# One written list of steps for the first batch of an attention and MLP kernel, and fewer transfers for v and the keys

## The chip, the cores and the metric

The kernel runs on one core of a Trainium2 chip. The metric is device microseconds of one execution, the median over runs. Lower is better. A profiled execution gives, besides its own time, a trace of every instruction of every engine: TensorE (PE; PEld is its weight load), VectorE (DVE), ScalarE (ACT), GpSimd (POOL), and SyncE (SP), which here only issues DMAs. A letter q behind an engine's name (SPq, POOLq) means the engine's own instruction queue issuing a DMA.

## The reference

Attention over q, k, v of shape (8 batches, 12 heads, 448 positions, 64), with each query and key row divided by its root mean square and multiplied by a gain, then a two-layer network with a tanh gelu over the 3584 x 768 result:

```python
def rmsnorm(x, g):
    rms = np.sqrt(np.mean(x * x, axis=-1, keepdims=True) + 1e-06)
    return x / rms * g
q_n, k_n = (rmsnorm(q, g_q), rmsnorm(k, g_k))
scores = (1.0 / np.sqrt(64)) * np.matmul(q_n, k_n.transpose(0, 1, 3, 2))
scores = scores - np.max(scores, axis=-1, keepdims=True)
attn = np.exp(scores)
attn = attn / (np.sum(attn, axis=-1, keepdims=True) + 1e-09)
attn_out = np.matmul(attn, v)
x = attn_out.transpose(0, 2, 1, 3).reshape(3584, 768)
h = x @ w_in                                    # w_in 768 x 2048
g = 0.5 * h * (1.0 + np.tanh(c * (h + 0.044715 * h * h * h)))
out = g @ w_out                                 # w_out 2048 x 768
```

Inputs and output are float32; the kernel multiplies in bfloat16. Instead of each row's maximum it subtracts a constant (`shift`) that it computes from the gains.

## The kernel before, in words

The order of the instructions of every engine is the order in which the code emits them (`manual_schedule`, L69); each engine takes its own in that order, and waits for others come from the tiles that instructions share. A tile that is taken from a pool waits until everything that uses the pool's same buffer before it is over.

**Units.** A batch's 12 heads form six pairs, two heads to a pair (`head`, L103), and two pairs form one of three chunks. A chunk's queries and keys come in one raw tile each (`load_q`, `load_k`, L106 and L122, SP issues, six DMAs in all). 448 keys make three full tiles of 128 keys for each pair and a rest of 64 keys; the rests of the two pairs of a chunk share one tile ("r"). So a batch has 21 score tiles. Before, each pair's heads have 256 keys (four to a partition) on their own 64 partitions and 192 keys (three to a partition) on the other 64 (`halves`, L117). v goes the same way through POOL with a cast to bfloat16 (`load_v`, L139): three DMAs for each half of the heads, where the third (`vr`) writes the rest rows once more into a tile of their own.

**A pair's way.** Squares (L164, on ACT or POOL), totals along the 64 columns (DVE, L192), reciprocal root on ACT (`rsqrt`, L195, a logarithm and an exponential), normalization (L209, on DVE or POOL), transposition on PE into a PSUM tile (`trans`, L221), copies to `qT` and `kT` (DVE); or, for later batches, transposition by DMA (L248) and a gain on DVE (L260). Then `scores` (L265): two matmuls and one exponential of ACT for each tile. `pair_products` (L306) with what=0 gives the sums of exponentials (by a weight of ones), with what=1 the product with v. `pair_recips` (L326) transposes the sums on DVE, takes the reciprocal and transposes back; `pair_x` (L335) multiplies into `xT`.

**PSUM.** Three tiles of two banks (`ps_s`, for scores and pairs of first-layer blocks), one bank `ps_o` (`bank`, for sums and products), one bank `ps_m` (for transpositions, single first-layer blocks, and the second layer).

**First batch.** Loads, memsets and 16 idle matmuls on zeros (L620), the first pair's steps written out (L621 to L650), then `first_attention` (L514): a loop over the 21 tiles, with steps hung on tile numbers in four plans (`side`, `mid`, `early`, `late`, L661 to L680). Sums and products of a pair take turns in the one bank of `ps_o`. At its end `first_blocks` (L496) mixes the last pair's sums with the first first-layer blocks, calls `between0` (L701: the rest of batch 1's totals, its reciprocal roots in one go, and the load of the gelu table), and the remaining blocks of the first layer (`mm1`, L349) follow; between them batch 1 is normalized on DVE, pairs 0, 1, 4 and 5 are transposed on PE and chunk 1 by DMA (plan `m1`, L713).

**Later batches.** `attention` (L451) runs batch b + 1 in seven groups of three tiles, each filled up with steps of the second layer of batch b (`FILLS`, 96 steps after the first batch, the first 48 of which need the first half of `wout` alone); then `first_blocks` and the first layer of batch b + 1, while batch b + 2 is loaded, squared, normalized on POOL and transposed by DMA. POOL issues the weights' loads (`w_in_part`, two halves; `w_out_part`, two halves). Raw tiles have four buffers for each kind; a placeholder tile is taken once (L565).

## Time and profile before

| what | us |
|---|---|
| median of 3 runs (range) | 434.73 (434.52 to 435.49) |
| profiled execution, its own time | 437.02 |
| its span, first to last instruction | 434.9 |
| PE / ACT / DVE / POOL busy in the span | 414.1 / 286.1 / 265.4 / 160.6 |
| 0 to 100 us: PE busy, mean of ten stages | 83.8 of 100 |
| 100 to 435 us: PE busy | 330.3 of 335 |

The span is what the trace covers; sums over the trace are made against it. The share of busy time is a mean over stages with different limits: the first 100 us and the rest have to be read apart. A line of the timeline gives start, duration, engine, source line, operation, output and inputs with shapes, how many are merged, and in brackets the idle time before and what ended it. DMA moved at 178 to 242 GB/s in each of the first eight stages of 10 us and at 124 to 131 between 150 and 250 us. Loads issued at 25 to 31 us took 16.4 to 16.8 us to land, those of the first 4 us between 2.4 and 4.0.

### The profile page before, as it was taken

What the parts mean: (1) busy time and instruction counts of PE and PEld (TensorE: products, weight loads), DVE (VectorE), ACT (ScalarE), POOL (GpSimd) and SP (SyncE); (2) the same over time, 40 slices, a digit from 0 to 9 for tenths busy, and PEclk for the clock granted to TensorE, in tenths of its full rate; (3) what the DMA queues carried; (4) which work ended last, traced back from release to release, by engine and by line L of the source; (5) the groups of instructions that cost most, each with busy time, mean ns of one, the idle gap of its engine ahead of it and who ended that gap; (6) DMA issues with size and microseconds to landing.
All of it is one profiled execution on the core that took longest, in us unless ns stands there. A gap on an engine that the chain in (4) does not pass through costs nothing.

```text
span 434.9 us, 9265 instructions
## 1 busy us (share of the span) xinstructions
PE 414.1 (95%) x3776; PEld 236.4 (54%) x3776; DVE 265.4 (61%) x441; ACT 286.1 (66%) x382; POOL 160.6 (37%) x181
## 2 busy tenths in 40 slices
PE   8778798899999999999999999999999999999996
PEld 3234454456555565556465655556565655556563
DVE  5577846798667844787267845877377821784010
ACT  5676538366787758767786859777786648674400
POOL 4979223254660094205560194206560280000000
PEclk9899999699999999999999999999999999999999
DMA  7999999665895158913994168914991162120022
GB/s 177 217 228 233 231 179 230 124 110 95 206 194 107 38 128 170 217 51 73 208 186 102 38 150 160 217 43 78 220 142 39 38 110 56 36 69 7 2 72 72
DMA packets 90505, 54.92 MB, mean 126 GB/s; under 512 B 51808, under 2 KB 85472, under 8 KB 90464
## 3 DMA queue, kind: packets, MB, share of 16 engines
q1 hardware_dynamic: 65248, 41.67, 42.9%
q0 software_dynamic: 24896, 12.59, 21.9%
q8 instruction: 29, 0.48, 0.4%
q10 hardware_dynamic: 320, 0.10, 0.1%
q14 instruction: 12, 0.10, 0.1%
HBM read 47.19 MB, written 11.01 MB: 134 GB/s over the span
## 4 chain that ended last, share of the span: by engine, by line
PE 79%; DMA 13%; DVE 5%; SPq 2%; issue 1%; ACT 0%; DVEq 0%
PE o L386 32%; PE hh L362 26%; PE o L321 10%; PE sc L285 6%; DMA rawk<-in_k_dram 6%; DMA rawq<-in_q_dram 4%; PE h L362 3%; DMA kT<-nrmk 3%; PE sc L275 1%; SPq L129 1%; DVE ss L193 1%; DVE es L301 1%; DVE es L299 1%; SPq L110 1%; DVE nrmq L216 0%
## 5 line engine op out<-in xcount | busy, mean ns | idle before, releaser
L386 PE MATMUL o<-wout,g 128*64 128x384 bf16 (+1 forms) x1664 | 159.7, 329 | 0.0
L289 ACT ACTIVATE ex<-sc,shift 128x896 bf16<-128x896 f32 x144 | 136.6, 1013 | 8.5 <-PE sc L285 8.4
L362 PE MATMUL hh<-xT,win 128*64 128x448 bf16 (+1 forms) x960 | 135.3, 355 | 2.7 <-ACT g L368 2.6
L386 PEld LDWEIGHTS <-g 128*64 128x64 bf16 (+1 forms) x1664 | 99.4, 110 | 50.6 <-issue 4.6
L362 PEld LDWEIGHTS <-win 128*64 128x64 bf16 (+1 forms) x1098 | 88.1, 106 | 61.5 <-issue 8.2
L368 ACT ACTIVATE g<-hh 128x896 bf16<-128x896 f32 x56 | 49.6, 917 | 55.0 <-PE hh L362 55.0
L193 DVE TENSOR_REDUCE ss<-sq 112x16 f32<-112x1024 f32 (+4 forms) x44 | 46.8, 1077 | 39.9 <-ACT sq L176 32.7
L408 ACT COPY osb<-o 128x384 f32<-128x384 f32 x51 | 24.7, 485 | 59.5 <-PE o L386 59.5
L331 DVE STREAM_TRANSPOSE st<-o 128x448 f32<-128x448 f32 x48 | 31.2, 649 | 29.4 <-PE o L321 29.3
L654 POOL COPY mark<-es 1x1 bf16<-1x1 bf16 x6 | 1.1, 178 | 127.0 <-DVE es L301 127.0
L216 POOL TENSOR_TENSOR nrmq<-rawq,rinv 112x512 bf16<-112x512 f32 x40 | 41.7, 1060 | 3.1 <-ACT rinv L202 3.1
L285 PE MATMUL sc<-qT,kT 64*128 64x448 bf16 x288 | 38.6, 355 | 1.4 <-DVE kT L243 0.9
L321 PE MATMUL o<-ex,vb 128*64 128x448 bf16 x288 | 36.9, 363 | 1.0 <-DVE st L331 0.8
L301 DVE TENSOR_TENSOR es<-ex 128x896 bf16<-128x896 bf16 x42 | 27.7, 659 | 15.4 <-ACT ex L289 15.2
L216 POOL TENSOR_TENSOR nrmk<-rawk,rinv 128x384 bf16<-128x384 f32 (+1 forms) x40 | 36.8, 936 | 0.0
L338 DVE TENSOR_TENSOR xT<-o,rb 128x448 bf16<-128x448 f32 x48 | 29.6, 617 | 4.4 <-PE o L321 3.5
L178 POOL TENSOR_TENSOR sq<-rawq 112x1024 f32<-112x1024 f32 x9 | 17.4, 1929 | 39.9 <-DMA rawq<-in_q_dram 25.8
L333 DVE STREAM_TRANSPOSE rb<-rc 128x448 f32<-128x448 f32 x48 | 31.0, 645 | 1.6
L299 DVE TENSOR_TENSOR es<-es,exr 64x896 bf16<-64x896 bf16 x42 | 27.4, 653 | 3.0 <-ACT exr L289 1.6
L301 DVE TENSOR_TENSOR es<-es,ex 128x896 bf16<-128x896 bf16 x42 | 27.1, 645 | 2.4 <-ACT ex L289 0.3
L261 DVE TENSOR_SCALAR kT<-kT,gcol 128x896 bf16<-128x896 bf16 x19 | 15.4, 813 | 21.4 <-DMA kT<-nrmk 21.4
L289 ACT ACTIVATE exr<-sc,shift 128x896 bf16<-128x896 f32 x24 | 24.5, 1021 | 0.2 <-PE sc L275 0.2
(71 smaller groups left out, 318.4 us busy)
## 6 DMA issues: line engine op xcount, KB each, us to landing
rawq<-in_q_dram SPq DMA_DIRECT2D x48, 224.0 KB, 4.2
rawk<-in_k_dram SPq DMA_DIRECT2D x48, 128.0 KB, 4.5
rawk<-in_k_dram SPq DMA_DIRECT2D x48, 96.0 KB, 4.4
vb<-in_v_dram POOLq DMA_DIRECT2D x16, 192.0 KB, 6.0
win<-in_moe_w_in_dram POOLq DMA_DIRECT2D x2, 1536.0 KB, 16.9
wout<-in_moe_w_out_dram POOLq DMA_DIRECT2D x2, 1536.0 KB, 21.8
out_dram<-osb SPq DMA_DIRECT2D x7, 336.0 KB, 3.9
vb<-in_v_dram POOLq DMA_DIRECT2D x16, 144.0 KB, 6.7
```

The lines of the kernel that those rows point to most:

```text
L193: nc.vector.reduce_sum(stat(ssq[b % 3], b, c, n, j), view(n, sqs[n, b, c], j), axis=AX.X)
L216: eng.tensor_mul(dst.rearrange("p t a d -> p a t d"), view(n, raws[n, b, c], j), r.to_broadcast(list(r.shape) + [D]),)
L285: nc.tensor.matmul(sc[:, a, :S], kT[r, c, 4 * j + t], qT[b][r, hp], start=True, stop=True,)
L289: nc.scalar.activation(dst, sc[:, :, :S], AF.Exp, scale=scale, bias=shift)
L299: nc.vector.tensor_add(es[p], es[p], exrs[b, hp // 2][p])
L301: nc.vector.tensor_add(es, ex[:, 0] if t == 1 else es, ex[:, t])
L321: nc.tensor.matmul(o[a * D:(a + 1) * D], w(a), e[:, a], start=(i == 0), stop=(i + 1 == len(steps)),)
L331: nc.vector.transpose(st.rearrange("p a b -> p (a b)"), oas[0])
L333: nc.vector.transpose(oas["rb"], rc.to_broadcast([128, S // 32, 32]))
L362: nc.tensor.matmul(h[i * m:(i + 1) * m, j, :S], win[:, c // 2 + NCH * (c % 2), f * 128 + i * m:f * 128 + (i + 1) * m], xT[b][:, c], start= ...
L368: nc.scalar.activation(g[:, fs[0]:fs[0] + len(fs), (b % 2) * S:(b % 2 + 1) * S], h[:, :, :S], AF.Gelu_apprx_tanh)
L386: nc.tensor.matmul(o[j * m:(j + 1) * m, :HD], g[:, f, i * 128 + j * m:i * 128 + (j + 1) * m], wout[:, f, half * HD:(half + 1) * HD], start ...
```

## The change

Five things change, all in the code above; from the attention of batch 2 on only the loads of v and keys differ.

1. **Keys.** For each pair one DMA of 384 keys, three to each of 128 partitions, and one of the last 64 keys on 64 partitions; still four key DMAs to a chunk. The order in a chunk is queries, main keys, queries, main keys, rest, rest for every chunk of every batch. Which keys lie in which tile changes with it.
2. **v.** One DMA for 384 rows of all 12 heads and two for the rests, instead of six; rest rows are no longer written twice.
3. **First batch as a list.** `first_attention`, its plans and `between0` go away. A string names each step in the order in which it is emitted, for all engines together: `sq0:A` is the query square of pair 0 on ACT, `tq` `tk` totals, `rs` reciprocal root, `nq` `nk` normalization, `tp` transposition, `cq` `ck` copies, `s` and `e` score matmuls and exponential of a tile, `z` idle matmuls, `su` sums, `st` `rc` `rb` the three steps of the reciprocals, `xp` product with v, `xt` multiplication, `v` and `w` loads of v and of quarters of w_in, `o` loads of w_out (two quarters and a half), `L` loads of queries and keys, `ma` `mc` `md` first-layer blocks over pairs 0 to 3, 4, 5 (or all), `g` gelu; capitals are batch 1, by chunk for `Sq` `Sk` `Tq` `Tk` `Rs`. A, D and P are ACT, DVE and POOL.
4. **PSUM in the first batch.** Sums stay in `ps_o`, products go to `ps_m`, transpositions of pairs 1 to 5 go to `ps_s`, those of batch 1 to `ps_o`. Scores and their exponential are separate steps, first-layer blocks and their gelu as well. Before the second pair's sums there are 11 idle matmuls.
5. **Batch 1.** Only chunk 0 is normalized and transposed in the list; the roots of chunks 1 and 2 come after the exponential table is loaded. Chunk 1 is normalized on DVE and transposed on PE in the first two groups of its attention, chunk 2 is normalized on POOL and transposed by DMA there, and `loads(2, 1)` and `loads(2, 2)` stand behind these DMAs on SP. Squares of batch 2 move to groups 1 to 3, v of batch 2 to group 3.

All squares of the first batch now lie in the space of the hidden activations; two placeholder tiles of raw data are taken instead of one.

```diff
    vb = [wts.tile([128, NCH, 2, NS, D], BF16, name=f"vb{i}") for i in range(2)]
-    vr = [wts.tile([128, 2, NCH, 2, D], BF16, name=f"vr{i}") for i in range(2)]
+    vb = [wts.tile([128, H, NK, D], BF16, name=f"vb{i}") for i in range(2)]
...
     def load_k(b, c):
         t = rawqk.tile([128, 2, NS, D], F32, tag="rawk", name="rawk")
         raws["k", b, c] = t
 
-        def go(j):
+        def main(j):
             h = head(c, j)
-            for p, s, n, at in halves(j):
-                nc.sync.dma_start(
-                    t[p, :, at:at + n],
-                    k[b, h:h + 2, s].rearrange("a (p t) d -> p a t d", t=n),
-                )
-        return [lambda j=j: go(j) for j in range(2)]
+            nc.sync.dma_start(
+                t[:, :, 4 * j:4 * j + NK],
+                k[b, h:h + 2, :SM].rearrange("a (p t) d -> p a t d", t=NK),
+            )
+
+        def last(j):
+            h = head(c, j)
+            nc.sync.dma_start(t[own(j), :, NK], k[b, h:h + 2, SM:].rearrange("a p d -> p a d"))
+        return [lambda: main(0), lambda: main(1), lambda: last(0), lambda: last(1)]
...
-        for go in load_q(b, c) + load_k(b, c):
+        lq, lk = load_q(b, c), load_k(b, c)
+        for go in (lq[0], lk[0], lq[1], *lk[1:]):
...
-    def load_v(b, j, cs=slice(0, NCH)):
-        src = v[b, HP * j + 2 * cs.start:HP * j + 2 * cs.stop]
-        dst, rem = vb[b % 2], vr[b % 2]
-        for p, s, n, at in halves(j):
+    def load_v(b, part):
+        if part == 0:
             nc.gpsimd.dma_start(
-                dst[p, cs, :, at:at + n].rearrange("p c a t d -> p (c a) (t d)"),
-                src[:, s].rearrange("h (p t) d -> p h (t d)", t=n),
+                vb[b % 2].rearrange("p h t d -> p h (t d)"),
+                v[b, :, :SM].rearrange("h (p t) d -> p h (t d)", t=NK),
             )
-        p, s, n, at = halves(j)[0]
-        nc.gpsimd.dma_start(
-            rem[p, j, cs].rearrange("p c a d -> p (c a) d"),
-            src[:, s].rearrange("h (p t) d -> p h t d", t=n)[:, :, 3 - 3 * j],
-        )
+        else:
+            j = part - 1
+            nc.gpsimd.dma_start(
+                vr[b % 2][own(j), j], v[b, HP * j:HP * j + HP, SM:].rearrange("h p d -> p h d")
+            )
...
-    def trans(b, hp):
+    def trans(b, hp, home=None):
 
         c, j = hp // 2, hp % 2
         if hp == 0:
             qT[b] = qkp.tile([128, HP, S], BF16, tag="qT", name="qT")
-        tp = ps_m.tile([128, 2, 512], BF16, tag="mm", name="tp")
+        pool, tag = home or (ps_m, "mm")
+        tp = pool.tile([128, 2, 512], BF16, tag=tag, name="tp")
         for t in range(NQ):
             nc.tensor.transpose(
                 tp[:, 0, t * P:(t + 1) * P],
                 nrms["q", b, c][:, j, t].rearrange("p a d -> p (a d)"), ident[:P, :P],
             )
...
+    def pair_products(b, hp, what, home=None):
 
         c, j = hp // 2, hp % 2
-        o = oas[what] = bank()[:, :S]
-        idle(waits, o)
+        o = oas[what] = (home or bank())[:, :S]
         main = [exs[b, hp][:, t] for t in range(NK)]
         if what:
-            steps = [(main[t], lambda a, t=t: vb[b % 2][:, c, a, 4 * j + t]) for t in range(NK)]
-            steps.append((exrs[b, c], lambda a: vr[b % 2][:, j, c, a]))
+            steps = [(main[t], lambda a, t=t: vb[b % 2][:, head(c, j) + a, t]) for t in range(NK)]
+            steps.append((exrs[b, c], lambda a: vr[b % 2][:, j, 2 * c + a]))
         elif b == 0:
...
+    TILES = [(2 * c + (n > 2), (0, 1, 2, "r", 0, 1, 2)[n]) for c in range(NCH) for n in range(NS)]
+    ENG = {"A": nc.scalar, "D": nc.vector, "P": nc.gpsimd}
...
+        elif name == "tp":
+            tps[0, i] = trans(0, i, (ps_s, "sc") if i else (ps_m, "mm"))
...
+        elif name == "z":
+            hp, m = divmod(i, 100)
+            if hp not in sums_at:
+                sums_at[hp] = bank()
+            idle(m, sums_at[hp][:, :S])
+        elif name == "su":
+            pair_products(0, i, 0, sums_at.get(i))
...
+        elif name == "xp":
+            pair_products(0, i, 1, ps_m.tile([128, 512], F32, tag="mm", name="ox"))
...
+        elif name == "o":
+            w_out_part(*((0, slice(0, 8)), (0, slice(8, 16)), (1,))[i])
...
+        elif name == "Tp":
+            tps[1, i] = trans(1, i, (ps_o, "o"))
...
+    FRONT = """
+        sq0:A sk0:A tq0 tk0 sq1:P gcol rs0 nk0:D sk1:A tq1 tk1 sq2:A nq0:D v0 rs1 tq2 sk2:A tp0
+        nk1:P tk2 z5 cq0:A ck0:D nq1:P rs2 shift sk3:A s0 sq3:P s1 sq4:D e0 tp1 tk3 nk2:P e1 tq3
+        s2 sk4:P z4 cq1:D e2 ck1:D v1 tk4 s3 s4 nq2:P rs3 sk5:D z2 e3 nk3:D nq3:P tp2 tk5 e4 s5
+        tq4 su0 sq5:P L10 e5 ck2:D cq2:D s6 v2 st0 s7 rs4 tp3 w0 rc0 e6 rb0 xp0 w1 ck3:D e7 s8 tq5
+        su1 nk4:P e8 cq3:D xt0 w2 s9 rs5 s10 st1 s11 nq4:P e9 xp1 rc1 rb1 e10 Sq0:P nq5:D tp4 xt1
+        e11 s12 cq4:D su2 ck4:D e12 w3 nk5:D s13 s14 Tq0 L11 L12 e13 Sk0:P tp5 xp2 cq5:D e14 ck5:D
+        s15 st2 s16 e15 s17 rc2 su3 rb2 e16 xt2 s18 st3 xp3 e17 rc3 rb3 s19 e18 s20 xt3 su4 e19
+        Tk0 xp4 e20 st4 ma0 rc4 Rs0 rb4 GELU Nq0:P xt4 su5 Nk1:P xp5 st5 Nk0:P rc5 mc0 rb5 Sq1:P
+        ma1 o0 xt5 Sk1:D mc1 Nq1:P md0 Tk1 o1 Tp0 g0 ma2 Tq1 Cq0:A Ck0:D L20 mc2 Sq2:A Tp1 Sk2:D
+        md1 md2 Ck1:A md3 g1 Cq1:D Tq2 g2 V0 V1 V2 Tk2 md4 g3 o2 md5 g4 md6 g5 md7 g6 md8 g7 g8
+"""
+    for step in FRONT.split():
+        front(step)
...
+            here = {(0, 0): [lambda j=j, n=n: normed(1, 1, n, j, nc.vector)
+                             for j in range(2) for n in "qk"] +
+                            [lambda: normed_all(1, 2), lambda: transposed(1, 2),
+                             lambda: loads(2, 1), lambda: loads(2, 2)],
+                    (1, 0): [lambda: transposed_here(1, 2)],
+                    (1, 1): [lambda: transposed_here(1, 3)]}
+            late = [(2, lambda: total(2, 0, "q")), (3, lambda: total(2, 0, "k"), lambda: gain(1, 2)),
+                    (4, lambda: total(2, 1, "q")), (5, lambda: total(2, 1, "k")),
+                    (6, lambda: total(2, 2, "q"), lambda: total(2, 2, "k"))]
+            for c in range(NCH):
                 for n in "qk":
-                    side.append((slot, lambda c=c, n=n: square(2, c, n, nc.gpsimd)))
+                    side.append((1 + c, lambda c=c, n=n: square(2, c, n, nc.gpsimd)))
...
+        if b == 0:
+            rsqrt(1, slice(1, NCH))
         if b + 2 < B:
-            side += [(0 if b else 2, lambda: load_v(b + 2, 0), lambda: load_v(b + 2, 1))]
+            side += [(0 if b else 3, *(lambda i=i: load_v(b + 2, i) for i in range(3)))]
```

More of the change, by code (lines that the diff above doesn't have):

```diff
@@ L622 @@
-    totals0(0)
-    rsqrt0(0)
-    for a in range(2):
-        nc.vector.tensor_mul(gcol[a * D:(a + 1) * D], grow[:, 0:1], grow[:, 1:2])
-    nc.vector.tensor_scalar(gdiag, ident[:D, :D], gcol[:D, 0:1], None, op0=ALU.mult)
-    gall = bank()
-    nc.tensor.matmul(gall[:, :D], rows, gdiag, start=True, stop=True)
-    idle(3, ps_m.tile([128, 512], F32, tag="mm", name="w")[:, :S])
-    square(0, 0, "q", nc.scalar, ("pair", 1))
-    normed0(0, nc.vector)
-    nc.vector.tensor_reduce(
-        shift, gall[:, :D], axis=AX.X, op=ALU.max, apply_absolute_value=True
-    )
@@ L638, with gains @@
[L638 to L650 removed]
+    def gains():
+        for a in range(2):
+            nc.vector.tensor_mul(gcol[own(a)], grow[:, 0:1], grow[:, 1:2])
+        nc.vector.tensor_scalar(gdiag, ident[:D, :D], gcol[:D, 0:1], None, op0=ALU.mult)
+        oas["gall"] = bank()
+        nc.tensor.matmul(oas["gall"][:, :D], rows, gdiag, start=True, stop=True)
+        idle(3, ps_m.tile([128, 512], F32, tag="mm", name="w")[:, :S])
```

326 lines of the change are left out of this document (148 added, 178 removed).

## The prediction, written before the changed kernel was run

> **What bounds the kernel now.** I read the granted clock and span first (one core, 434.9 us, 0.984), then the slices of the page, then stage windows, then the timeline of the first 112 us, the DMA queues and the waits. The slices:
>
> ```profile
> span 434.9 us, 9265 instructions
> PE   8778798899999999999999999999999999999996
> PEclk9899999699999999999999999999999999999999
> DMA  7999999665895158913994168914991162120022
> ```
>
> One digit is 10.9 us. TensorE is full from the ninth digit on; the holes are in the first eight, where DMA is full. The stages (columns: us of each engine, clock, DMA share, GB/s):
>
> ```profile
> 0.00:10.00 10.00, 8.04 (x37) 3.29 (x38) 5.23 (x18) 5.15 (x9) 3.92 (x15) 1.00 0.76 178
> 20.00:30.00 10.00, 8.06 (x64) 3.27 (x63) 6.41 (x13) 6.32 (x9) 8.22 (x9) 0.89 1.22 228
> 50.00:60.00 10.00, 7.80 (x38) 3.82 (x38) 5.60 (x11) 6.02 (x7) 0.00 (x0) 0.83 1.37 200
> 70.00:80.00 10.00, 6.65 (x64) 3.37 (x62) 9.77 (x11) 7.74 (x10) 4.15 (x2) 0.84 1.22 242
> 150.00:200.00 50.00, 50.00 (x491) 29.46 (x489) 32.58 (x55) 38.02 (x53) 19.22 (x21) 1.00 0.64 131
> ```
>
> After 101 us PE hides everything: 330.3 of the 335 us from 100 us on are PE time. So only what moves the start of that full stretch counts. The timeline gives its milestones:
>
> ```profile
> 9.50 1.01 ACT L289 ACTIVATE ex<-sc,shift 128x896 bf16<-128x896 f32 x1 [0.38 <-PE sc L285]
> ...
> 38.40 1.91 ACT L289 ACTIVATE ex<-sc,shift 128x896 bf16<-128x896 f32 x2 [0.58 <-PE sc L285]
> ...
> 46.61 0.95 ACT L176 ACTIVATE g<-rawk 128x896 f32<-128x896 f32 x1 [5.36 <-DMA rawk<-in_k_dram]
> ...
> 52.20 6.38 PE L362 MATMUL hh<-xT,win 128*128 128x448 bf16 x24 [2.57 <-ACT g L368]
> ...
> 66.76 0.74 PE L285 MATMUL sc<-qT,kT 64*128 64x448 bf16 x6
> ...
> 70.00 0.46 DVE L261 TENSOR_SCALAR kT<-kT,gcol 128x896 bf16<-128x896 bf16 x1 [3.48 <-DMA kT<-nrmk]
> ...
> 77.94 0.59 PE L321 MATMUL o<-es,ones 128*64 128x448 bf16 x2 [2.86 <-DVE es L299]
> ...
> 101.24 3.03 PE L362 MATMUL hh<-xT,win 128*64 128x448 bf16 x30
> ```
>
> First exponential at 9.50, the 21st over at 40.31; ACT waits 5.36 us for batch 1's last keys, so gelu starts late and PE idles 2.57 us; attention of batch 1 starts at 66.76; a transposing DMA holds DVE, so PE idles another 2.86 us; next first layer at 101.24. I price four stretches up to that point.
>
> **Change, stretch 1: to the first exponential.** Pair 0 needs two landings (queries, main keys) instead of three, which saves about one SP issue (0.60), but the list lets DVE do both totals of pair 1 before pair 0's query normalization and puts the key square of pair 3 on ACT ahead of the first exponential. That square needs the second chunk whole. Before, the last key piece of it was issued at 7.72 and took 4.3 (keys issued at 7 to 8.4): 12.0. Now POOL issues v after one square of 1.04, about 7.4, instead of at 9.79. While v ran beside it, the SP queue moved one 0.917 MB chunk between 12.0 and 17.9, that is 0.155 MB/us. Of chunk two 0.69 MB is left at 9.0 (its first queries landed at 8.80): 13.4, plus a square of 0.63: first exponential at 14.1. Bounds: 12.6 if v disturbs nothing, 15.6 if v takes half of the 0.23 MB/us. The key transposition that must also be over ends near 11.5; the five idle matmuls queued before the first scores wait, by the reuse of the one bank, for the shift at 11.75 and take up to 1.9 (five of 0.375), so scores come by 13.9: hidden. Cost **+4.6**.
>
> **Stretch 2: the 21 exponentials.** Before 40.31 - 9.50 = 30.8, of which ACT needs 21 x 0.955 (two in 1.91) plus reciprocal roots of 0.55 to 0.58 each; the rest were gaps, since sums and products took turns in one bank and the products waited for DVE's transposes (1.12 and 1.04 us gaps at L321 and L331). Now sums, products and transposes sit in different banks. Three roots and 21 exponentials: 21.8. Gaps I find by going through the list with the rows' durations: 0.45 before the fourth exponential (DVE is held by a query square that lands at 14.9), 0.8 for the fourth root (DVE is held by the chunk-three key square until about 19.2), 0.6 before the ninth, 0.35 in small ones: 24.0, end 38.1. PE (18 scores of 0.3, four transpositions of 0.75, ten sums or products of 0.88: 17.2 us) and DVE (19.8 us from the first sum's transpose) fit beside it, without much left: DVE's own end is 42.4. Cost **-6.8**; bounds 21.8 and the old 30.8.
>
> **Stretch 3: first layer.** Before 66.76 - 40.31 = 26.4. Now gelu waits only for the root of batch 1's first chunk (loaded by 24.1 before), so neither the 2.57 us hole nor the half-clock matmuls behind it (0.375 against 0.20 from 52.2 to 56.3, some 2 us) should come. PE work left after the 21st exponential: 96 first-layer products at 0.2025 (12 in 2.43) = 19.4, one sum and product 1.8, two transposition sets 1.5 (four before, two go to stretch 4): 22.7; attention 1 starts at 61.0 with 0.2 for handover. Squares moved to DVE, ACT and POOL lie under these matmuls (DVE 9 us, ACT 12 us of 23); if uncovered, they would cost what the old wait for batch 1 cost, 5.36. Cost **-3.5**.
>
> **Stretch 4: attention of batch 1.** Before 101.24 - 66.76 = 34.5. Chunk 1 is now transposed on PE, chunk 2 by DMA, first needed in the fifth group of seven. What is late next is weights: POOL reaches the two quarters of w_out near 45, then v, then the second half at 50 (before 40.28 to 46). From 45 to 55 us the POOL queue moved 1.52 MB in 10 us. First half 10.3 us: 55.8, in time. v: 2304 packets of 48.8 ns (15.9% of 16 engines over 46 us, 2400 packets) on 16 engines: 63. Second half: 73.3 at that pace, 75 with SP traffic beside it; it is first read in the fourth group. That group would start at 74.7 by PE and DVE (4.9 for group one, 8.6 for the next two), so about 75, and the old tail from 84.36 to 101.24 is 16.9: next first layer at 91.9. Cost 30.9 - 34.5 = **-3.6**.
>
> **Costed at nothing.** v in three issues instead of six: POOL's 4.2 us per batch become perhaps 2.4 (768 descriptors took 0.90, 2048 took 1.2); POOL is busy 19.2 of 47.7 us, nobody waits. The 0.1 MB of v that is no longer written twice is 0.5 us of DMA. Keys: per chunk 512 packets of 768 bytes and 256 of 256 instead of 512 of mean 896. At 3 to 8 us a packet of 859 bytes took 58 ns (88.3% of 16 engines, 1211 packets); at 150 to 196 us one of 576 took 40: 0.064 ns a byte, so 20 ns for 256 bytes. Over the seven chunks ahead of the last weights: 3584 x -8.2 + 1792 x 20 ns = 6 us on 16 engines, 0.4. Upper bound, 58 ns each: 4.7. I take 0.4, as the fit comes from packets that include small ones; w_out's slack covers it.
> The Trainium skill (DMA: Bandwidth & Descriptors, Specifications) speaks against this edit: transfers under 512 bytes lose line rate to read-modify-write. Charging 256 bytes like 512 (36 ns by the fit) would give an estimated 2.2 us of DMA, of which stretch 4 would show about 1.5; no row here isolates it.
>
> **Sum.** +4.6 - 6.8 - 3.5 - 3.6 = -9.3. I add 1.0 for handovers that the walk rounds off (21 tiles by 0.05): -8.3. Span 434.9 becomes 426.6; the median shown is 0.2 below that span (the profiled execution's own time, 437.02, is above it): **426.4**.
>
> **Rivals.**
> (a) The in-order lists hold each other and stretch 2 stays at 30.8: +6.8, and the allowance falls away: 432.2. For: three engines are at 70 to 90% there, and a list has no slack at a late landing. Against: the separate banks remove waits that the trace names.
> (b) The last weights decide. If the POOL queue gets only the 1.53 MB in 15 us of 60 to 75, the 3.83 MB from 45 end at 82.6, and 82.6 + 16.9 = 99.5: 433.0; halfway, 429.7. For: v stands before the second half. Against: SP has little to load then.
> (c) Slower: PE runs attention 0 at half clock. The list keeps 11 idle matmuls there, before there were 19, and PE waits about 2.4 us before the first transposition and again for the first key factors. The row at 52.20 shows that 2.57 us of idling bring 0.375 us matmuls. If this held from 14 to 38, PE's 17.2 us would become 34.4, the first layer would start near 52 instead of 38: -8.3 + 14 = +5.7, 440.4. It decides from about 17 us at half clock on. Against: 8.06 of 10 us busy at 20 to 30 gave clock 0.89, and the list keeps PE some 70% busy. The Trainium skill (TensorE: Matmul & The Clock Gate, Part 1) gives an idle window of about 3.4 us; the 2.57 us row fell sooner.
> (d) Data come smoothly and the allowance is not needed, nor the wait for weights: 421 to 424.
>
> **Chances.** Forecast 0.50 (423.5 to 429.5 by itself), (a) 0.17, (b) 0.12, (c) 0.16, (d) 0.05. What this kernel's measurement can tell from no change is about 0.2%, 0.9 us. (a) and (b) lie around 430 to 435, so I give 0.05 to no change: faster 0.79, same 0.05, slower 0.16. Range 421.5 to 434.5: it leaves out (c) and the best of (d).
>
> **What would show it.** First exponential near 14, 21st over near 38, attention 1's first scores near 61, its fourth group near 75, first layer of batch 1 near 92; no PE hole at the first gelu and no wait of L261's kind before group four. If the fourth group waits for wout, it is (b); if first-layer matmuls start after 43, (a); if the two score matmuls of a key tile take 0.6 us instead of 0.3, (c). Wrong altogether if the stretch after 101 us changes, which I hold fixed.

## The result

| what | before | after |
|---|---|---|
| median of 5 runs each, same chip, us | 434.52 (434.31 to 435.49) | 436.83 (436.07 to 437.65) |
| ratio to before, 95% interval | 1 | 1.0048 [1.003, 1.0067] |
| profiled execution, its own time, us | 437.02 | 436.07 |
| its span, us | 434.9 | 434.3 |

The change made the kernel half a per cent slower; 426.4 us was forecast. The two profiled executions mislead here: the one of before was 2.5 us above the median of its kernel, the one of after 0.8 us below. So the times are compared by medians, and the stages with a second profile of the kernel before (c_before, below).

The slices of the page of the changed kernel (40 slices of 10.9 us, busy tenths):

```profile
span 434.3 us, 9127 instructions
PE   5789994998999999999999999999999999999996
PEclk9899998899999999999999999999999999999999
DMA  7999999537996169923992177913981152120022
```

The first digit falls from 8 to 5, since the first exponential comes later. From the third to the fifth TensorE is fuller than it was (8, 9, 9 for 7, 8, 7). A new hole stands in the seventh, 65 to 76 us, a 4 where there was an 8: it lies in the attention of batch 1, and the clock falls with it (8 and 8).

The milestones, from the timelines (us):

| milestone | before, profiled | c_before | forecast | after |
|---|---|---|---|---|
| first exponential starts | 9.50 | 9.70 | 14.1 | 14.20 |
| 21 exponentials over | 40.31 | 40.48 | 38.1 | 38.16 |
| attention 1 starts | 66.76 | 66.93 | 61.0 | 59.79 |
| its fourth group starts | 84.36 | 81.80 | 75 | 80.84 |
| first layer of batch 1 starts | 101.24 | 98.69 | 91.9 | 99.12 |
| attention 2 starts | 119.82 | 117.28 | 110.5 | 119.30 |
| from there to the end of the span | 315.1 | 315.0 | 315.1 | 315.0 |

The forecast of 110.5 is 91.9 plus the old 18.6, which the prediction held fixed; it adds 1.0 of allowance behind that. Up to attention 1 the change did what was forecast, and 7 us were in hand. Against c_before all of them were lost within the next 60 us: it took 39.3 us instead of the forecast 30.9 to the first layer of batch 1, and 20.2 instead of 18.6 from there to the next attention.

The timeline of TensorE in the changed kernel, where they went:

```profile
59.79 0.74 PE L299 MATMUL sc<-qT,kT 64*128 64x448 bf16 x6
...
65.95 1.49 PE L405 MATMUL o<-wout,g 128*64 128x384 bf16 x16
71.87 0.37 PE L230 MATMUL tp<-ident,nrmq 112*128 112x112 bf16 x4 [4.44 <-DVE kT L255]
...
75.39 2.45 PE L405 MATMUL o<-wout,g 128*64 128x384 bf16 x14 [1.01 <-DVE kT L255]
...
99.12 3.03 PE L378 MATMUL hh<-xT,win 128*64 128x448 bf16 x30
...
104.64 0.76 PE L336 MATMUL o<-ex,vb 128*64 128x448 bf16 x6 [1.35 <-DVE st L343]
```

TensorE stands 4.44 us before the second transposition of chunk 1, because VectorE has not yet copied the first one into `kT`. Behind the wait 14 matmuls take 2.45 us; at 81.85, at full clock, the same 14 take 1.30. Here is what VectorE did meanwhile:

```profile
62.41 0.69 DVE L217 TENSOR_TENSOR nrmq<-rawq,rinv 112x512 bf16<-112x512 f32 x1 [11.40 <-ACT rinv L203]
63.02 0.55 DVE L217 TENSOR_TENSOR nrmk<-rawk,rinv 128x384 bf16<-128x384 f32 x1
63.49 4.33 DVE L217 TENSOR_TENSOR nrmq<-rawq,rinv 112x512 bf16<-112x512 f32 x1
67.74 0.68 DVE L217 TENSOR_TENSOR nrmk<-rawk,rinv 128x512 bf16<-128x512 f32 x1
68.34 0.61 DVE L317 TENSOR_TENSOR es<-ex 128x896 bf16<-128x896 bf16 x1
69.06 2.13 DVE L317 TENSOR_TENSOR es<-es,ex 128x896 bf16<-128x896 bf16 x1
71.11 0.38 DVE L246 COPY qT<-tp 128x448 bf16<-128x448 bf16 x1
71.41 0.40 DVE L255 TENSOR_SCALAR kT<-tp,gcol 128x384 bf16<-128x384 bf16 x1
71.74 1.47 DVE L317 TENSOR_TENSOR es<-ex 128x896 bf16<-128x896 bf16 x1
```

And GpSimd, over the same microseconds:

```profile
62.46 3.01 POOL L217 TENSOR_TENSOR nrmq<-rawq,rinv 112x512 bf16<-112x512 f32 x2 [12.56 <-ACT rinv L203]
65.44 1.83 POOL L217 TENSOR_TENSOR nrmk<-rawk,rinv 128x384 bf16<-128x384 f32 x2
67.24 3.47 POOL L179 TENSOR_TENSOR sq<-rawq 112x1024 f32<-112x1024 f32 x1
70.67 2.06 POOL L179 TENSOR_TENSOR sq<-rawk 128x896 f32<-128x896 f32 x1
```

The same normalization takes VectorE 0.69 us once and 4.33 us the next time, with no wait in brackets: the instruction has started, and is held. It is freed about when the four normalizations of GpSimd end, at 67.27. Then VectorE runs three operations and GpSimd's square needs 3.47 us, where the same square of before at 62.18, with VectorE idle for most of it, took 1.88; then VectorE's addition needs 2.13 instead of some 0.6, beside that same square, then another 1.47. The two engines take turns on a resource. It is no new thing in this kernel: in the profile of before the addition at 73.21 took the same 2.13 us beside a square of GpSimd.

```profile
72.63 2.23 POOL L178 TENSOR_TENSOR sq<-rawq 112x1024 f32<-112x1024 f32 x1 [6.92 <-DVE ss L193]
73.21 2.13 DVE L301 TENSOR_TENSOR es<-es,ex 128x896 bf16<-128x896 bf16 x1
```

Both rows stood in the profile from which the prediction was made, and the duration of the addition was not asked after. The Trainium skill (SBUF — State Buffer, Who interferes with whom) states what the rows show: VectorE and GpSimd share a port pair under an exclusive lock, and a VectorE instruction with two inputs in SBUF contends with a GpSimd instruction that reads SBUF. All the rows named are of that kind, and none of the copies from PSUM (0.38 to 0.40 us) is stretched.

### The profile page after: what moved, and what is told of

It reads as the page before. It is cut to its first block, busy times and chain, and to the rows that moved or that the text cites. A ratio compares the mean times of both kernels' runs of the same rounds, so it can differ in the third digit from the quotient of the medians.

```text
span 434.3 us, 9127 instructions
## 1 busy us (share of the span) xinstructions
PE 410.2 (94%) x3732; PEld 232.5 (54%) x3732; DVE 265.6 (61%) x436; ACT 287.4 (66%) x387; POOL 154.6 (36%) x160
## 4 chain that ended last, share of the span: by engine, by line
PE 80%; DVE 8%; DMA 6%; ACT 2%; issue 1%; SPq 1%; DVEq 0%; ACTq 0%
PE o L405 31%; PE hh L378 27%; PE o L336 10%; DMA rawk<-in_k_dram 6%; PE sc L299 6%; PE h L378 4%; DVE ss L194 2%; DVE es L317 1%; PE sc L289 1%; DVE nrmq L217 1%; ACT ex L303 1%; DVE st L343 1%; DVE rb L351 1%; DVE es L315 1%; DVE kT L255 0%
## 5 line engine op out<-in xcount | busy, mean ns | idle before, releaser
L378 PE MATMUL hh<-xT,win 128*64 128x448 bf16 (+1 forms) x924 | 133.0, 353 | 0.0
L378 PEld LDWEIGHTS <-win 128*64 128x64 bf16 (+1 forms) x1062 | 85.9, 105 | 59.2 <-issue 3.2
L194 DVE TENSOR_REDUCE ss<-sq 112x16 f32<-112x1024 f32 (+1 forms) x42 | 47.6, 1148 | 44.6 <-ACT sq L177 31.9
L217 POOL TENSOR_TENSOR nrmq<-rawq,rinv 112x512 bf16<-112x512 f32 x44 | 46.9, 1081 | 23.9 <-ACT rinv L203 15.2
L217 POOL TENSOR_TENSOR nrmk<-rawk,rinv 128x384 bf16<-128x384 f32 (+1 forms) x43 | 39.8, 942 | 1.7 <-ACT rinv L203 1.7
L179 POOL TENSOR_TENSOR sq<-rawq 112x1024 f32<-112x1024 f32 x10 | 20.5, 2052 | 43.1 <-DMA rawq<-in_q_dram 29.7
L336 PE MATMUL o<-ex,vb 128*64 128x448 bf16 x252 | 31.8, 359 | 1.9 <-DVE st L343 1.9
L315 DVE TENSOR_TENSOR es<-es,exr 64x896 bf16<-64x896 bf16 x42 | 25.9, 617 | 2.7 <-ACT exr L303 1.3
L361 DVE TENSOR_TENSOR xT<-o,rb 128x448 bf16<-128x448 f32 x42 | 25.9, 616 | 2.8 <-PE o L336 2.0
L299 PEld LDWEIGHTS <-kT 64*128 64x128 bf16 x288 | 10.2, 94 | 27.4 <-issue 17.1
```

The costliest lines, as they stand in the source:

```text
L194: nc.vector.reduce_sum(stat(ssq[b % 3], b, c, n, j), view(n, sqs[n, b, c], j), axis=AX.X)
L217: eng.tensor_mul(dst.rearrange("p t a d -> p a t d"), view(n, raws[n, b, c], j), r.to_broadcast(list(r.shape) + [D]),)
L299: nc.tensor.matmul(sc[:, a, :S], kT[r, c, 4 * j + t], qT[b][r, hp], start=True, stop=True,)
L315: nc.vector.tensor_add(es[p], es[p], exrs[b, hp // 2][p])
L336: nc.tensor.matmul(o[a * D:(a + 1) * D], w(a), e[:, a], start=(i == 0), stop=(i + 1 == len(steps)),)
L378: nc.tensor.matmul(h[i * m:(i + 1) * m, j, :S], win[:, c // 2 + NCH * (c % 2), f * 128 + i * m:f * 128 + (i + 1) * m], xT[b][:, c], start= ...
```

## The experiments

Each kernel is compared with runs of the kernel before on the same chip. The theory after the comparison of the two traces was: **port** (the normalizations of VectorE and GpSimd hold each other, and TensorE pays), with **clock** (the wait matters because TensorE is at half clock behind it), **transfers** (the new loads cost, or bring batch 2 too late) and **late totals** (sums of batch 2's squares stand ahead of the last pair's reciprocals) as rivals or further shares.

### c_before: the kernel before once more

> The kernel before, unchanged, to see a second profile of it. The first profiled execution took 437.02 us where its median is 434.5, so its span of 434.9 us may be about 2 us longer than a usual one. Theory A (the profiled execution was a slow one): a span of 432.3 to 433.0 and a first layer of batch 1 that starts near 99 instead of 101.24. Theory B (it was usual, and the changed kernel loses its gain elsewhere): 434.9 and 101.2 again. Ratio 1.000 +- 0.002 in both.

435.87 us against 436.05, ratio 1.0001 [0.9977, 1.0025], span 432.3. Its milestones are within 0.2 us of those of the first profile up to the third group of attention 1, where the first profile lost 2.7 us more (10.7 us for 8.0), 1.7 of them in one wait of TensorE:

```profile
76.45 0.38 PE L321 MATMUL o<-es,ones 128*64 128x448 bf16 x2 [1.20 <-DVE es L299]
```

1.20 us here, 2.86 in the profile shown of before, at the same matmuls. The wait is for the first of two additions of VectorE. The pair in the first profile:

```profile
75.79 2.74 DVE L299 TENSOR_TENSOR es<-es,exr 64x896 bf16<-64x896 bf16 x2
```

and in c_before:

```profile
75.79 1.26 DVE L299 TENSOR_TENSOR es<-es,exr 64x896 bf16<-64x896 bf16 x2
```

In the first profile a square of GpSimd ran beside them, from 75.48 to 77.41; in c_before that square began at 76.45, when the first addition was over. So the two executions of one kernel differ by the same hold that costs the changed kernel its gain. What follows: the baseline against which the sum was made was some 2.6 us later from that point on than in this execution. Times like that of the first profile are not rare, though: of the 38 executions of this kernel on the chip of c_before, 14 took 436.5 us or more, and the one profiled here, 434.47, lies 1.5 under their median. Where the others lost their time was not profiled. Against c_before the changed kernel loses 0.4 us up to the first layer of batch 1 and 1.6 more up to attention 2, and these 2.0 us are the whole difference of the spans, 434.3 to 432.3.

### e_loads_alone: the kernel before with nothing but the new transfers

The edit, in short:

```diff
-                for p, s, n, at in halves(j): ...            # keys: two pieces per half
+                t[:, :, 4 * j:4 * j + NK], k[b, h:h + 2, :SM]  # one main piece per half
+                t[own(j), :, NK], k[b, h:h + 2, SM:]           # and a small one
-    load_v(b, j)      # j in 0, 1: three issues each
+    load_v(b, part)   # part in 0, 1, 2: one issue each
```

> The kernel before with only the new transfers of v and keys. My prediction charged them 0.4 us: 434.5 to 435.5. If small key packets cost what the page's rule gives, 2 us, it is 436 to 437, and then the transfers are what made the changed kernel slower.

435.9 us, ratio 1.0002 [0.9976, 1.0028]. The transfers cost nothing that can be measured in the old kernel, and bring nothing: as a cost the rival **transfers** falls.

### e_list_old_loads: the list, with the old transfers

The converse of the edit above, made in the changed kernel: keys and v loaded in the old pieces, `v0 v1` and `V0 V1` for `v0 v1 v2` and `V0 V1 V2`.

> The changed kernel with the old transfers of v and keys. If the list alone decides, 436 to 437.5, as the changed kernel; if the new transfers cost 2 us, 434 to 435; if the new transfers were a gain, 438 or more.

440.3 us, ratio 1.0106 [1.0075, 1.0138]. Slower than the whole change by some 0.6%, with intervals that do not meet, though from different groups of runs. So by these medians the new transfers are worth something in the list and nothing that shows outside it. Where is not shown: in the profile attention 1 starts at 62.90 us instead of 59.79, TensorE having waited 2.23 us for a normalization of GpSimd at 20.48 with a granted clock of 0.66 between 20 and 30 us; but single executions of the list with the new transfers start their first layer as late (last section).

### e_pool_waits: GpSimd starts its normalizations when VectorE's are done

```diff
-                            [lambda: normed_all(1, 2), lambda: transposed(1, 2),
+                            [lambda: gpsimd_waits(nrms["k", 1, 1][:1, NK, 0, :1]),
+                             lambda: normed_all(1, 2), lambda: transposed(1, 2),
```

> The changed kernel, but in batch 1's attention GpSimd waits for the last normalization of chunk 1 on VectorE before it normalizes chunk 2. Port theory (a VectorE operation with two SBUF inputs is held while GpSimd works through a series of its own): the 4.33 us normalization takes 0.7 and the second transposition of that attention starts 2 to 4 us earlier than 71.9; some of it may come back as longer additions of exponentials. 1 to 4 us faster than 436.8. Late-data theory (chunk 1 or its roots come too late): no change, 436.8.

437.74 us, ratio 1.0058 [1.0034, 1.0082]: no gain. The timeline of VectorE in this kernel tells why:

```profile
64.28 0.69 DVE L217 TENSOR_TENSOR nrmq<-rawq,rinv 112x512 bf16<-112x512 f32 x1 [11.39 <-ACT rinv L203]
64.89 0.55 DVE L217 TENSOR_TENSOR nrmk<-rawk,rinv 128x384 bf16<-128x384 f32 x1
65.36 0.69 DVE L217 TENSOR_TENSOR nrmq<-rawq,rinv 112x512 bf16<-112x512 f32 x1
65.96 0.69 DVE L217 TENSOR_TENSOR nrmk<-rawk,rinv 128x512 bf16<-128x512 f32 x1
66.56 0.62 DVE L317 TENSOR_TENSOR es<-ex 128x896 bf16<-128x896 bf16 x1
67.29 7.71 DVE L317 TENSOR_TENSOR es<-es,ex 128x896 bf16<-128x896 bf16 x1
```

And of GpSimd:

```profile
67.19 2.04 POOL L217 TENSOR_TENSOR nrmq<-rawq,rinv 112x512 bf16<-112x512 f32 x2
69.19 1.83 POOL L217 TENSOR_TENSOR nrmk<-rawk,rinv 128x384 bf16<-128x384 f32 x2
70.99 1.88 POOL L179 TENSOR_TENSOR sq<-rawq 112x1024 f32<-112x1024 f32 x1
72.84 1.67 POOL L179 TENSOR_TENSOR sq<-rawk 128x896 f32<-128x896 f32 x1
```

With GpSimd idle, all four normalizations of VectorE take 0.55 to 0.69 us. GpSimd then runs six operations at full speed from 67.19 to 74.51, and the one addition of VectorE that began 0.1 us after it is held through all six: 7.71 us. TensorE waits 6.37 us for `kT` instead of 4.44 (attention 1 had also begun 1.9 us later, at 61.66). As proof of the mechanism this is the clearest run; as a remedy it failed, because the waiting was moved to the next instruction with two inputs in SBUF and drawn together there. The expectation had allowed for longer additions, but not that one of them would take back the whole gain.

### e_norm_dve: VectorE normalizes chunk 2 as well, GpSimd none of batch 1's last chunks

```diff
-                            [lambda: normed_all(1, 2), lambda: transposed(1, 2),
+                            [lambda j=j, n=n: normed(1, 2, n, j, nc.vector)
+                             for j in range(2) for n in "qk"] +
+                            [lambda: transposed(1, 2),
```

> The changed kernel with chunk 2 of batch 1 normalized on VectorE too, behind chunk 1, so that GpSimd has no series of operations in the first two groups of that attention (its squares of batch 2 then run under the first layer, since nothing holds them back). Port theory: every normalization takes 0.55 to 0.7 us, every addition of exponentials 0.6; 2.5 us of VectorE work is added and about 7 us of being held goes away: attention 1 shortens by 2 to 4 us, 433 to 435 where the changed kernel has 436.8 (ratio 0.996 to 1.001). If VectorE's own amount of work decides, attention 1 gets longer by up to 2.5.

431.58 us against 435.01, ratio 0.9915 [0.9898, 0.9932], span 429.3: faster than both kernels, by 0.9% than the one before and by 1.3% than the changed one (0.9915 over 1.0048, from two groups of runs). The same work was given to the busier of the two engines. In the stages of 10 us (engines' busy time, then clock, share of the DMA engines, GB/s), the changed kernel between 70 and 80 us:

```profile
70.00:80.00 10.00, 6.85 (x48) 3.33 (x50) 7.81 (x14) 2.80 (x3) 2.73 (x2) 0.66 1.01 247
```

and e_norm_dve:

```profile
70.00:80.00 10.00, 8.93 (x103) 5.08 (x100) 9.32 (x18) 5.99 (x7) 1.89 (x1) 1.00 1.03 225
```

103 matmul records instead of 48, clock 1.00 instead of 0.66. TensorE's wait before the second transposition, 4.44 us in the changed kernel, is here:

```profile
69.64 0.37 PE L230 MATMUL tp<-ident,nrmq 112*128 112x112 bf16 x4 [1.56 <-DVE kT L255]
```

The second and third groups of attention 1 take 10.65 us (65.12 to 75.77) instead of 16.36 (64.48 to 80.84), so the port, with the half clock that follows its waits, cost 5.7 us, and the first layer of batch 1 starts at 94.10 instead of 99.12. The eight normalizations take VectorE some 5 us in all, less than four took beside GpSimd. GpSimd's squares of batch 2's first chunk, which had stood behind its normalizations, ran at 50.80 to 54.33, under the first layer, and met nobody. From that layer to attention 2 it is still 20.2 us: the late totals are another matter.

### e_keep_warm: 16 idle matmuls inside the wait

```diff
-                    (1, 1): [lambda: transposed_here(1, 3)]}
+                    (1, 1): [lambda: idle(16, bank()[:, :S]), lambda: transposed_here(1, 3)]}
```

> The changed kernel with 16 idle matmuls (3.2 us at full clock) in the 4.4 us that TensorE waits before the second transposition of batch 1's attention. Half-clock theory (much of the loss is that the matmuls behind the wait run at 0.37 instead of 0.19): no half-clock stretch at 72 to 79, the third group takes 5 to 6.5 us instead of 8.4, 2 us faster. Port theory alone: the wait itself stays, and the third group is held by VectorE's steps: less than 0.7 us.

436.98 us, ratio 1.0036 [1.0021, 1.0051]. TensorE now waits 1.13 us ahead of the idle matmuls, and its clock is full when the first tiles come, but the third group still takes 8.2 us (72.89 to 81.06) instead of 8.4. VectorE's rows are those of the changed kernel, 4.33 and 2.13 us among them. So keeping TensorE busy in that wait is worth a few tenths. But the half clock was only moved: behind another wait for `kT`, of 1.21 us, the granted clock is 0.58 from 76 to 78 us and 0.57 from 78 to 80:

```profile
75.90 2.08 PE L405 MATMUL o<-wout,g 128*64 128x384 bf16 x14 [1.21 <-DVE kT L255]
```

The same 14 matmuls take 1.30 us at full clock. What the matmuls of the third group take longer than the same rows in e_norm_dve, at full clock, adds up to some 1.8 us here and 2.7 in the changed kernel. **Clock** therefore falls as a loss of its own, since the waits before it come from VectorE; its share in the 5.7 us was not separated.

### e_sq_early and e_root_early: the squares of batch 2, then batch 1's roots, under the first layer

The edit of e_sq_early, abridged:

```diff
-        ... md4 g3 o2 md5 g4 md6 ...
+        ... md4 g3 o2 md5 g4 Yq0:P Yk0:P Uq0 Uk0 md6 ...
-            late = [(2, lambda: total(2, 0, "q")), (3, lambda: total(2, 0, "k"), lambda: gain(1, 2)), ...
+            late = [(2, lambda: total(2, 1, "q")), (3, lambda: total(2, 1, "k"), lambda: gain(1, 2)),
+                    (4, lambda: total(2, 2, "q")), (5, lambda: total(2, 2, "k"))]
```

> The changed kernel with the squares and totals of batch 2's first chunk moved from groups 2 to 4 of batch 1's attention to the end of the list, where GpSimd and VectorE idle from 51 to 62 us; the other chunks' totals move up by two groups, as they were before the change. Port theory: the additions held for 2.13 and 1.47 us fall to 0.6, the 4.33 us normalization stays; totals no longer stand before the last pair's reciprocals (1.35 us of PE wait at 104.64 goes away): 2 to 4 us faster than the changed kernel, ratio 0.995 to 1.000. If neither matters: 1.0048 as before.

433.97 us, ratio 0.9971 [0.9954, 0.9988]. With the squares of the first chunk of batch 2 gone from GpSimd's series, VectorE's third normalization takes 2.53 us and the addition 1.07; the third group ends at 76.90. But the fourth group then takes 8.6 us, since a total of the next chunk stands on VectorE and waits for a square whose queries land only then:

```profile
79.68 1.22 DVE L194 TENSOR_REDUCE ss<-sq 112x16 f32<-112x1024 f32 x1 [2.98 <-POOL sq L179]
```

GpSimd had waited 7.00 us for that load. From the first layer to attention 2 it took 18.59 us: with no total ahead of the last reciprocals the 1.6 us are back.

The edit of e_root_early against e_sq_early, abridged (the same steps go from attention 1):

```diff
+        elif name == "Rv":
+            nc.scalar.preload_act_table_set(EXP_SET)
+            rsqrt(1, slice(1, NCH))
+            nc.scalar.preload_act_table_set(GELU_SET)
-        ... md4 g3 o2 md5 g4 Yq0:P ...
+        ... md4 g3 Rv Nq4:D Nk4:D Nq5:D Nk5:D X2 o2 Nq2:D Nk2:D Nq3:D Nk3:D md5 g4 Yq0:P ...
```

> A version meant to beat both: as e_sq_early, and the roots of chunks 1 and 2 are taken in the middle of the first layer (two more table loads of 1.28 us on ACT, which idles 1.35 us between gelus there), so that all normalizations of batch 1 and the DMA transposition of chunk 2 are over before its attention starts. If what I put the lost 8 us down to is right (VectorE held by GpSimd, the PE wait and the half clock behind it), attention 1 takes 30 to 33 us instead of 39.3 and the time is 428 to 431 (ratio 0.985 to 0.992). If data come late instead, a wait appears at its first groups and less than 3 us are won.

432.55 us, ratio 0.9927 [0.9903, 0.9951], no more than e_norm_dve brings. All eight normalizations lie under the first layer here, and the third group starts at 69.20. The second and third groups take 8.98 us (65.98 to 74.96). The fourth is held for the same reason as in e_sq_early: TensorE waits 1.10 us behind a total whose square waits for its load; in the fifth it waits 1.69 us, behind the next total and an addition that took 1.28 us beside a square of GpSimd. The expectation (428 to 431) had not seen that batch 2's data are then the next thing late.

### e_norm_totals and e_totals_alone: the totals one group earlier

The first is e_norm_dve, the second the changed kernel, each with

```diff
-            late = [(2, lambda: total(2, 0, "q")), (3, lambda: total(2, 0, "k"), lambda: gain(1, 2)),
-                    (4, lambda: total(2, 1, "q")), (5, lambda: total(2, 1, "k")),
-                    (6, lambda: total(2, 2, "q"), lambda: total(2, 2, "k"))]
+            late = [(1, lambda: total(2, 0, "q")), (2, lambda: total(2, 0, "k")),
+                    (3, lambda: total(2, 1, "q"), lambda: gain(1, 2)), (4, lambda: total(2, 1, "k")),
+                    (5, lambda: total(2, 2, "q"), lambda: total(2, 2, "k"))]
```

(in the second both totals of chunk 0 stand in slot 2). Slots count from 0: slot 1 is the second group.

> e_norm_dve with the totals of batch 2's squares one group earlier (chunk 0 after the second and third groups, chunk 1 after the fourth and fifth, chunk 2 after the sixth), so that none stands ahead of the last pair's reciprocals. In e_norm_dve the two totals of chunk 2 take 2.21 us on VectorE at 96.8, and the next attention begins 20.2 us after the first layer of batch 1 (18.6 in the kernel before). Theory (the price of the late totals is a wait of TensorE of 1.35 us behind the reciprocals, a separate loss from the port): 18.6 to 19.0 us from that first layer to the next attention, whole span 1.2 to 1.6 us under e_norm_dve's 429.3, ratio to before 0.988 to 0.990. Rival (VectorE's work is the limit of groups five to seven, so that what is moved ahead lengthens them by as much): the first layer begins 1 to 2 us later than 94.1 and the ratio stays at 0.9915. Rival (the root for batch 2, which waits for these totals, is what decides the next attention, through the normalizations behind it): the same gain, but the wait ahead of the next attention's first transpositions falls, not the one at the reciprocals.

> The changed kernel with nothing but the totals of batch 2's squares earlier (chunk 0 after the third group, chunk 1 after the fourth and fifth, chunk 2 after the sixth); the normalizations stay shared between VectorE and GpSimd. Theory (two separate losses: the port in the third group, the late totals behind the reciprocals): the third group ends as late as in the changed kernel (80.8), and the next attention begins 18.6 to 19.0 us after the first layer of batch 1 instead of 20.2, so 1.0 to 1.6 us off the changed kernel, ratio to before 1.001 to 1.003. Rival (the totals are late because the squares are, behind the port): the totals wait for GpSimd's squares in the third to sixth groups, these grow by 1 to 2 us, and the ratio stays at 1.004 to 1.006.

Both missed. 434.97 us, ratio 0.998 [0.996, 1.0001], and 440.04 us, ratio 1.011 [1.0091, 1.013]. From the first layer to attention 2 both take 18.58 us, as forecast by the theory; but the attention before it grew by more: 37.2 us against 33.7 in e_norm_dve, 43.0 against 39.3 in the changed kernel. Nearest came the first rival of e_norm_totals, that VectorE is the limit there; but it named the fifth to seventh groups and 1 to 2 us, and of the 3.5 us 2.7 fell in the third group. The timeline of VectorE in e_norm_totals:

```profile
73.75 1.22 DVE L194 TENSOR_REDUCE ss<-sq 112x16 f32<-112x1024 f32 x1
74.88 0.38 DVE L246 COPY qT<-tp 128x448 bf16<-128x448 bf16 x1
75.18 0.47 DVE L255 TENSOR_SCALAR kT<-tp,gcol 128x512 bf16<-128x512 bf16 x1
```

and of TensorE:

```profile
75.71 1.49 PE L405 MATMUL o<-wout,g 128*64 128x384 bf16 x14 [2.07 <-DVE kT L255]
```

A total of 1.22 us stands ahead of the copies of the transposed tiles, TensorE waits 2.07 us, and the third group takes 8.3 us instead of 5.6. In e_totals_alone it is the fifth group that grows, by 3.1 us (8.4 for 5.3): there a total stands on VectorE ahead of the gain on chunk 2's `kT`, and TensorE waits 2.21 us for it. In both, the totals of chunk 2 now stand ahead of the fifth pair's reciprocals, where TensorE waits 1.54 us instead of 0.41. So the late totals do cost 1.6 us where they are, and have no free place one group earlier. In e_norm_totals another 2.4 us were lost ahead of attention 1 (62.85 us instead of 60.43), in code that the edit did not touch; see the last section.

## Why the prediction was wrong

**Stretch 1, +4.6: the number right by luck, its reason not.** First exponential at 14.20, forecast 14.1. But the key square that was to decide, on the timeline of ScalarE in the changed kernel:

```profile
12.09 0.63 ACT L177 ACTIVATE g<-rawk 128x512 f32<-128x512 f32 x1 [0.61 <-DMA rawk<-in_k_dram]
14.20 2.80 ACT L303 ACTIVATE ex<-sc,shift 128x896 bf16<-128x896 f32 x3 [1.48 <-PE sc L299]
```

It was over at 12.7, not 14.0; the exponential waited 1.48 us for the scores, behind the five idle matmuls (11.64 to 13.66), which were priced "hidden", with the scores due at 13.9.

**Stretch 2, -6.8: right** in this execution, 23.96 us for 24.0, end 38.16 for 38.1. In other executions of the same code the gain is smaller (last section).

**Stretch 3, -3.5: right in its mechanism**, and -4.8 in fact: 21.6 us for 22.9, its end at 59.79 for 61.0. No hole at the first gelu, and the moved squares lay under the matmuls.

**Stretch 4, -3.6: the step that failed.** Forecast 30.9 us, measured 39.3. Group one took 4.69 for 4.9. Groups two and three were forecast at 8.6 "by PE and DVE" (61.0 + 4.9 + 8.6 is 74.5; the fourth group was put at "about 75", which leaves them 9.1), and took 16.36: this is the error, 7.3 us of the 8.4. GpSimd has no term in that sum: chunk 1 on VectorE and chunk 2 on GpSimd were taken to lie side by side at no cost to each other. e_norm_dve takes the collision away with one edit and these groups fall to 10.65, so 5.7 us of the error are the port and what follows its waits, shown. The 1.6 left over, 10.65 for 9.1, point to the normalizations that VectorE itself does there: in e_root_early, where none is left in attention 1, the two groups take 8.98. From the fourth group to the first layer it took 18.3 for 16.9, in e_norm_dve as well, so not by the hold in the third group. Of these 1.4 us, 1.0 fell in the fifth group (5.30 us, 4.34 in c_before):

```profile
86.64 0.36 PE L299 MATMUL sc<-qT,kT 64*128 64x448 bf16 x2 [0.78 <-DVE kT L275]
```

The gain on chunk 2's `kT` runs on VectorE at 86.15, right behind a total of 1.07 us. In the old kernel it was chunk 1 that was transposed by DMA, and its gain was over before the second group. That the order on VectorE is the cause is argued; no run moved the gain alone. The other 0.4 fell in the seventh group, where TensorE waits 0.60 us for an addition instead of 0.17. What the prediction named as late next, the weights, was not: no wait for `wout` stands in the fourth to seventh groups. Rival (b) falls.

**Held fixed: the stretch after 101 us.** The prediction said that it would be wrong altogether if that changed. It changed by 1.6 us, through the two totals at the end of the seventh group's list of `late` steps (slot 6), which the diff shows and the walk stopped short of. Four runs without a total in that place have 18.58 or 18.59 us there. On VectorE in the changed kernel:

```profile
101.83 2.21 DVE L194 TENSOR_REDUCE ss<-sq 112x16 f32<-112x1024 f32 x2
103.95 0.64 DVE L343 STREAM_TRANSPOSE st<-o 128x448 f32<-128x448 f32 x1
```

The transpose of the last pair's sums, which the 1.35 us wait of TensorE is for, stands behind them.

**Costed at nothing: right as far as the runs show.** The small packets of the keys cost nothing that shows in e_loads_alone: 4.7 us of time, the upper bound, are excluded, since its interval ends at 1.0028, 1.2 us. The rule of the Trainium skill (DMA: Bandwidth & Descriptors, Specifications) that transfers under 512 bytes lose rate would by the estimate made from it have shown about 1.5 us, a ratio of 1.0034, outside the interval too; but that estimate was made for the list, and in the list the new transfers as a whole gained.

**The base.** Span 434.9 was made into a median 0.2 lower, because before's happened to lie so. In every execution profiled the time is some 1.7 to 2.2 us above its own span (437.02 to 434.9, 436.07 to 434.3); the profiled one was simply a long one. A forecast span of 426.6 was 428.4 us in time, and 2.7 of the 34.5 us against which stretch 4 was set are not there in the execution of c_before. The prediction also put the 2.86 us wait down to a transposing DMA that holds VectorE. In c_before VectorE waits nearly as long for that DMA (3.19 us for 3.48), and TensorE waits 1.20: at least 1.7 of the 2.86 us were the same hold by GpSimd, already in the old kernel.

**Sum.** Forecast span 426.6, measured 434.3, 7.7 more: -1.2 from the stretches up to attention 1, +8.4 in stretch 4, +1.6 behind it, -1.0 for the allowance that was not needed, 7.8 in all. Of the rivals, (a) did not come (the stretch ended at 38.16, not 45); (b) did not, (c) came in part in some executions and not in this one; the slower side came by a mechanism that none of them named. Nor does the row at 52.20, on which (c) rests, make a rule: in the changed kernel TensorE stood idle for 2.81 us before 22.74, longer than the 2.57 there, and its next two matmuls took 0.36 us, at a granted clock of 1.00.

## What to carry to other kernels

Two elementwise streams on VectorE and GpSimd are not two lanes: before work is split between them, ask the old profile for a VectorE row with two SBUF inputs that lies beside a GpSimd row and compare its duration with the same row alone; here 2.13 us against 0.6 stood there before the change. Giving the whole piece to the faster engine beat sharing it, by 1.3%, and making one wait for the other only moved the hold to the next such instruction. And a baseline for a sum by stages wants two profiled executions of the old kernel: a wait that differs between them, here 2.86 and 1.20 us, is not safely the change's to win, and asking why it differs would have found the hold.

## What the runs showed that was not expected

**A hold lasts for a series.** VectorE was held not for one instruction of GpSimd but to the end of a series of four (4.33 us) and of six (7.71 us), as long as GpSimd always had its next one ready. In e_sq_early the hold ended earlier within a like series (2.53 us), so who wins at the boundary between two instructions is not settled by these runs.

**Identical code, 3 us apart.** Up to about 40 us the changed kernel and seven of its variants run the same list with the same loads. The first matmul of the first layer comes at 38.09 us in the changed kernel, 38.61 in e_keep_warm, 38.74 in e_norm_dve, 39.59 in e_root_early, 39.62 in e_sq_early, 39.75 in e_totals_alone, 39.97 in e_pool_waits and 41.16 in e_norm_totals; the granted clock of 10 to 20 and 20 to 30 us goes with it roughly. e_norm_totals:

```profile
10.00:20.00 10.00, 6.58 (x36) 2.59 (x36) 4.04 (x11) 5.93 (x11) 6.07 (x8) 0.77 1.19 214
20.00:30.00 10.00, 8.22 (x55) 3.02 (x54) 7.58 (x16) 5.97 (x10) 9.25 (x11) 0.72 1.06 197
```

and the changed kernel:

```profile
10.00:20.00 10.00, 8.30 (x57) 3.30 (x56) 6.07 (x13) 7.62 (x13) 9.00 (x10) 0.83 1.25 230
20.00:30.00 10.00, 6.75 (x65) 3.05 (x65) 9.86 (x21) 7.57 (x13) 9.26 (x9) 1.00 1.25 208
```

0.72 against 1.00 in the second stage. In the first, a wait of TensorE for `kT` at about 18 us lasted 2.53 us in e_norm_totals; in the changed kernel no wait from 15 to 19 us exceeds 0.21. The two that reached the first exponential soonest (12.29 us in e_pool_waits, 12.67 in e_norm_totals) were the ones that lost most afterwards. That is rival (c) on a small scale: in the five latest of these executions the gain of the list up to the first layer, some 1.6 us against c_before (38.09 to 39.73), is all but eaten up or lost altogether. Each kernel was profiled once and no run was made to remove it, so whether it goes with the execution, the chip or the build, and what decides it, stays open.
